# The first v load behind the first pair's q, and block sums spread by a sum over one number

## The chip, the cores and the metric

The kernel runs on one core of a Trainium2 chip. The metric is device time in microseconds (us) from launch to end, as the median of several runs. Beside it there is the profile of one execution, whose span counts from the first to the last instruction; the launch around it is not in the span.

The engines go by their names in the profile: PE is TensorE (PEld its weight loads), DVE is VectorE, ACT is ScalarE, POOL is GpSimd, SP is SyncE. SP, ACT and POOL issue the transfers (DMAs). Each engine works through its own instructions in their order and waits at semaphores for the others.

## The reference

Attention over blocks, and behind it an MLP mixer. q, k and v are 4 batches x 8 heads x 768 rows x 64. Of each head, the keys are cut into 12 blocks of 64, and a query attends to its own block and to the three blocks with the highest gate scores, causally:

```python
k_rep = k.reshape(B, H, n_blocks, block, D).mean(axis=3)
gate_scores = np.einsum('bhsd,bhnd->bhsn', q, k_rep)
...
top_idx = np.argsort(gate_scores, axis=-1)[..., -top_k:]
...
scores = np.where(mask, scores, -1000000000.0)
...
return np.matmul(attn, v).astype(np.float32)
```

The heads stand side by side as x, 768 x 512 for each batch. A token mixer follows (`h = relu(xt @ w_tok1) @ w_tok2`, `u = x + h^T`) and a channel mixer (`u + relu(u @ w_ch1) @ w_ch2`).

## The kernel before, in words

The work is done by pairs of heads, 16 in all (`pair(p)`, L482), four to a batch; behind each four come the two big products of the channel mixer (`mlp(b)`, L815). A pair goes through these steps:

- **Loads.** k and q of a pair, as f32, by SP; for pair 0 half of them by ACT, and in two halves of the rows (L516). v by POOL (L525), which makes f16 of it on the way, into the tile VA. A buffer of VA is one of five.
- **k.** TensorE transposes it (L446, `transposed`), VectorE sums each block of 64 columns (L553, `tensor_reduce` over a tile in PSUM) into ks3, 12 sums for each of the 64 numbers of a head. `spread` (L532 to L534) copies these sums, for each of the two heads, into ks2b, where a head's sums stand in columns of their own with zeros elsewhere; it is two copies of 64 partitions x 12 (pair 0: four of 64 x 6). The planner gives them to DVE or to POOL. From pair 6 on (`thirds`) `split` does this in another way, and `spread` is not used.
- **q.** TensorE transposes it (L446), ACT or DVE writes QT from PSUM (L342 or L344, the two lines of the helper `copy`), in two halves, (QT, 0) and (QT, 1). An f16 copy goes to QA (L344, L342).
- **Gate.** TensorE multiplies QT with ks2b (L639), VectorE adds the causal bias (L643), takes the greatest (L670) and compares (L683), and the own block is set by a memset (L690). What comes out, bn, is transposed (L710) and copied as 12 more rows into QA.
- **Scores and output.** L731 multiplies KA with QA, L744 (ACT) takes the exponential E, L752 (POOL) masks the diagonal blocks, L761 multiplies with VA.
- **Mixers.** L779 and L793 the token mixer, L827 and L849 the channel mixer.

No order of instructions is written by hand. Each step is given to a planner (`Plan`, L88) with its cost on each engine that could do it, what it reads and writes, and a due time `pr`. `Plan.run` (L129) is a list scheduler: it starts what can start first, by its own clock, and among what can start within 30 ns of that the one with the lowest `pr`. A transfer is not started until the planner's own count of the transfers under way is within 3 us (`AHEAD`) of being through, and not while another with a lower `pr` could go. The due times come from the table `L` (L53): for k, q and v of the first four pairs `ekd`, `eqd` and `evd`, taken from the pair's time `T(p) + L["o" + p]`. For pair 0 that time is -2.69, for pair 1 it is 5.78 + 2.1 = 7.88, for pair 2 it is 11.56 + 2.23. The instructions are then written out in the order of the planned starts, and it is that order by which each engine goes; when an instruction really starts is settled on the chip by its semaphores. Where TensorE would stand idle early on, the planner puts in filler matmuls on zeros (L899), their number fixed at build time.

The load of v has no input but its buffer, so in the program nothing but its place on POOL holds it back:

```python
P.op({"POOL": (1100.0, 2200.0, 1536 * 16.0 / 16)}, lambda: nc.gpsimd.dma_start(...),
     wr=[(VA, 0)], pr=t0 - lead["vd"], not_before=5000.0)
```

`not_before` is a bound of the planner's clock alone. `warm` is a tile of one number for each partition, which ACT writes once at the start (L520).

Of the kernel before, what the change touches and what calls it, by code (L numbers as in the profile page):

```python
# [13 lines left out]
ALU = mybir.AluOpType  # L14
AX = mybir.AxisListType
# [284 lines left out]
def kernel(  # L300
# [11 lines left out]
    nc = tc.nc  # L312
    B, H, S, D = q.shape
# [20 lines left out]
    def sb(shape, dt, name):  # L334
        return sp.tile(shape, dt, tag=name, name=name)
# [10 lines left out]
    P = Plan()  # L346
    ENG = {"PE": nc.tensor, "ACT": nc.scalar, "DVE": nc.vector, "POOL": nc.gpsimd, "SP": nc.sync}
# [39 lines left out]
    warm = sb([128, 1], FP, "warm")  # L387
# [40 lines left out]
    def weights(after):  # L428
        weight("w1", w1, moe_w_tok1.rearrange("(j p) t -> p j t", p=128), 768, 60, L["w1"], after)
        weight("w2", w2, moe_w_tok2.rearrange("(g p) s -> p g s", p=128), 256, 135, L["w2"], after)  # L430
        for c in range(NCC):
            weight(("wc1", c), wc1[:, c, :], moe_w_ch1[128 * c:128 * c + 128, :], 128, 247, L["wc1"] + c, after)
        for f in range(0, NFC, 3):
            weight(("wc2", f), wc2[:, f:f + 3, :], moe_w_ch2[128 * f:128 * f + 384, :].rearrange("(g p) c -> p g c", p=128),
                   384, 98, L["wc2"] + f / 3, after)


    def T(p):
        return EARLY * min(p, PPB) + PACE * max(0, p - PPB)
# [24 lines left out]
    def halves(i):  # L464
        return slice(HS * i, HS * i + HS)

    def upper(t):

        return t.bitcast(BF).rearrange("c (n two) -> c n two", two=2)[:, :, 1]
# [12 lines left out]
    def pair(p):  # L482
        b, c = divmod(p, PPB)
        h = 2 * c
        step = T(p + 1) - T(p)
        t0 = T(p) + L[f"o{p}"]
        thirds = p >= L["th"]
        cut = p < CUT
        lead = {n: L["e" + n if p < PPB else n] for n in LEADS}
# [5 lines left out]
        def at(i, lead):  # L495

            return t0 - lead - (L["cu"] if cut and i == 0 else 0.0)

        def loaded(t, i):
            return [(t, (x, i)) for x in range(2)] if cut else [(t, f) for f in range(4)]  # L500
        q32, k32 = Buf(q32r), Buf(k32r)
        qs, ks_, vs = q[b, h:h + 2], k[b, h:h + 2], v[b, h:h + 2]
        QA, KA, VA, QT = Buf(QAr), Buf(KAr), Buf(VAr), Buf(QTr)
        for t, src, name in ((k32, ks_, "kd"), (q32, qs, "qd")):
            e = "SP"
            if straight_k if t is k32 else straight_q:
                for f in range(4):
                    P.op({e: (570.0, 1600.0, 768 * 13.0 / 16)}, lambda f=f, t=t, src=src, e=e: ENG[e].dma_start(
                        out=t.t.rearrange("p j x d -> p (j x d)")[32 * f:32 * f + 32].rearrange("t (g i) -> t g i", i=32),
                        in_=src[f // 2, :, 32 * (f % 2):32 * (f % 2) + 32].rearrange("(g t) i -> t g i", t=32)), wr=[(t, f)], pr=t0 - lead[name])  # L510
                continue
            for x in range(2):
                e = "ACT" if p == 0 and x else "SP"
                for i in range(1 + cut):
                    n = NJ // (1 + cut)
                    P.op({e: (520.0 if p == 0 else 570.0, 1600.0, 128 * n * 17.6 / 16)}, lambda x=x, t=t, src=src, e=e, i=i, n=n: ENG[e].dma_start(  # L516
                        out=t.t[:, n * i:n * i + n, x, :], in_=src[x, 128 * n * i:128 * n * i + 128 * n].rearrange("(j p) d -> p j d", p=128)),
                        wr=[(t, (x, i) if cut else x)], pr=t0 - lead[name] - (199.0 - 20.0 * i + lead[name] if p == 0 else 0.0))
        if p == 0:
            P.op({"ACT": (1500.0, 1600.0)}, lambda: nc.scalar.activation(out=warm, in_=zero[:, 0:1], func=AF.Exp), pr=-98.0)  # L520
        if p < 3:
            e = "SP" if p else "ACT"
            P.op({e: (450.0, 1600.0, 24 * 135 / 16)}, lambda e=e: ENG[e].dma_start(out=KA.t[64:KR], in_=indc), wr=[(KA, "ind")],
                 pr=t0 - lead["qd"] + 0.2 if p else -99.0)
        P.op({"POOL": (1100.0, 2200.0, 1536 * 16.0 / 16)}, lambda: nc.gpsimd.dma_start(  # L525
            out=VA.t[:, :, :, 0:64], in_=vs.rearrange("x (j p) d -> p x j d", p=128)), wr=[(VA, 0)], pr=t0 - lead["vd"], not_before=5000.0)


        ks2b = kp = Buf(kppr if thirds else ksr)
        ks3 = Buf(ks3r)  # L530

        def spread(e, z):  # L532
            for x in range(2):
                ENG[e].tensor_copy(out=ks2b.t[64 * x:64 * x + 64, x, z], in_=ks3.t[64 * x:64 * x + 64, 0, z])  # L534

        if straight_k:
            KT = Buf(KTr)
            for i in range(2):
                P.op({"DVE": (487.0, 570.0)}, lambda i=i: nc.vector.transpose(
                    out=KT.t[:, halves(i)], in_=k32.t.rearrange("p j x d -> p (j x d)")[:, halves(i)]), rd=loaded(k32, i), wr=[(KT, i)], io="S0>S0", pr=t0 - L["ku"])  # L540
            P.op({"DVE": (862.0, 945.0)}, lambda: nc.vector.tensor_reduce(
                out=ks3.t[:, 0], in_=KT.t.rearrange("c (n w) -> c n w", w=64), axis=AX.X, op=ALU.add), rd=[(KT, 0), (KT, 1)], wr=[(ks3, 0), (ks3, 1)], io="S0>S0", pr=t0 - lead["kr"])
# [3 lines left out]
            if not thirds:  # L546
                P.op({"POOL": (380.0, 450.0), "DVE": (160.0, 240.0)}, lambda e: spread(e, slice(0, NB)), rd=[(ks3, 0), (ks3, 1)], wr=[(ks2b, 0), (ks2b, 1)], pr=t0 - lead["kr"] + 0.1, io="S0>S0 S2>S2")
        else:
            k16 = Buf(k16r)
            for i in range(2):  # L550
# [3 lines left out]
                    out=ks3.t[:, 0, 6 * i:6 * i + 6], in_=t.t[:, 0:HS].rearrange("c (n w) -> c n w", w=64),  # L554
                    axis=AX.X, op=ALU.add), rd=[(t, 0)], wr=[(ks3, i)], io="P0>S0", pr=at(i, lead["kr"]))
                if not thirds and (cut or i == 1):
                    z = slice(6 * i, 6 * i + 6) if cut else slice(0, NB)
                    P.op({"POOL": (380.0, 450.0), "DVE": (160.0, 240.0)}, lambda e, z=z: spread(e, z), rd=[(ks3, i)] if cut else [(ks3, 0), (ks3, 1)],
                         wr=[(ks2b, i)] if cut else [(ks2b, 0), (ks2b, 1)], pr=at(i, lead["kr"]) + 0.1, io="S0>S0 S2>S2")
# [17 lines left out]
        if dual:  # L577
            k16 = Buf(k16r)
            P.op({"POOL": (778.0, 828.0)}, lambda: nc.gpsimd.tensor_copy(
                out=k16.t.rearrange("p (j c) -> p j c", c=128), in_=k32.t.rearrange("p j x d -> p j (x d)")), rd=loaded(k32, 0), wr=[(k16, 0)], io="S0>S0", pr=t0 - L["k16"])  # L580
# [13 lines left out]
        for i in range(2):  # L594
            if straight_q:
                P.op({"DVE": (487.0, 570.0)}, lambda i=i: nc.vector.transpose(
                    out=QT.t[:, halves(i)], in_=q32.t.rearrange("p j x d -> p (j x d)")[:, halves(i)]), rd=loaded(q32, i), wr=[(QT, i)], io="S0>S0", pr=t0 - L["qu"])
# [7 lines left out]
            if thirds:  # L605
                a, z = (128, HS) if i == 0 else (HS, S)
                P.op(dve(z - a), lambda t=t, i=i, a=a, z=z: nc.vector.tensor_tensor(
                    out=R1.t[:, a - 128:z - 128], in0=t.t[:, a - HS * i:z - HS * i], in1=upper(QT.t[:, a:z]), op=ALU.subtract),
                    rd=[(t, 0), (QT, i)], wr=[(R1, i)], io="P0S0>S0", pr=t0 - L["r"])
        if straight_q and thirds:  # L610
            P.op({"POOL": (1207.0, 1257.0), "DVE": (745.0, 828.0)}, lambda e: ENG[e].tensor_tensor(
                out=R1.t, in0=QT.t[:, 128:S], in1=upper(QT.t[:, 128:S]), op=ALU.subtract), port=True, rd=[(QT, 0), (QT, 1)], wr=[(R1, 0), (R1, 1)], io="S0>S0", pr=t0 - L["r"])
        if p == 0:
            weights((QT, 0))
        for x in range(2):
            for i in range(1 + cut):
                n = NJ // (1 + cut)
# [12 lines left out]
        if not thirds:  # L630
            if cut:
                P.op({"POOL": (100.0, 150.0)}, lambda: nc.gpsimd.memset(gm.t[:, 0:2].rearrange("p j (x n) -> p j x n", n=NB)[:, :, :, 6:NB], -1.0e9), wr=[(gm, 9)], pr=t0 - lead["g"] - 9.0)
            for i, (z0, z1) in enumerate(parts):
# [3 lines left out]
                def gate(z0=z0, z1=z1, nb=nb):  # L637
# [6 lines left out]
                    out=cols(gm.t[:, z0:z1]), in0=g.t[:, W2 * z0:W2 * z1].rearrange("p (j w) -> p j w", w=W2)[:, :, 0:2 * nb].rearrange("p j (x n) -> p j x n", n=nb),  # L644
                    in1=cols(gbias[:, z0:z1]), op=ALU.add), rd=[(g, i)] + ([(gm, 9)] if cut else []), wr=[(gm, i)], io="P0S0>S0", pr=at(i, lead["g"]) + 0.1)
        else:
            P.op({"POOL": (1207.0, 1257.0)}, lambda: nc.gpsimd.tensor_tensor(out=R2.t, in0=R1.t, in1=upper(R1.t), op=ALU.subtract),
                 rd=[(R1, 0), (R1, 1)], wr=[(R2, 0)], io="S0>S0", pr=t0 - L["r"] + 0.1)
# [9 lines left out]
            for i in range(3):  # L658
                P.op({"DVE": (202.0, 283.0)}, lambda i=i: nc.vector.tensor_tensor(out=gm.t, in0=gv(2 - i), in1=(gm.t if i else gbias), op=ALU.add),
                     rd=[(g, 0)], wr=[(gm, 0)], io="P0S0>S0", pr=t0 - lead["g"] + 0.1)  # L660

        for i, (z0, z1) in enumerate(parts):
# [10 lines left out]
            if thirds:  # L673
                P.op({"DVE": (92.0, 174.0)}, lambda z0=z0, z1=z1, third=third: nc.vector.tensor_copy(out=third(), in_=m8.t[:, z0:z1, :, 2:3]),
                     rd=[(m8, i)], wr=[(g, (3, i))], io="S0>P0", pr=at(i, lead["g"]) + 0.25)
# [17 lines left out]
        if p >= L["bd"]:  # L693
            bnt = Buf(bntr)
            P.op({"DVE": (487.0, 570.0)}, lambda: nc.vector.transpose(  # L695
                out=bnt.t.rearrange("p j x n -> p (j x n)"), in_=bn.t.rearrange("p j x n -> p (j x n)")), rd=bn_all, wr=[(bnt, 0)], io="S0>S0", pr=t0 - lead["b"])
# [24 lines left out]
        for x in range(2):  # L721
# [34 lines left out]
            def av(a=a, E=E, x=x):  # L756
# [8 lines left out]
                out=rc.t.rearrange("p n o -> p (n o)"),  # L765
                in_=a.t[:, 0:NJ * 65].rearrange("p (j d) -> p j d", d=65)[:, :, 64:65].rearrange("p n o -> p (n o)")),
                rd=[(a, 0)], wr=[(rc, 0)], io="P0>S0", pr=t1 + 1.3)
            P.op(dve(384), lambda a=a, rc=rc, x=x: nc.vector.tensor_tensor(  # L768
                out=xp.t[:, :, 64 * x:64 * x + 64], in0=a.t[:, 0:NJ * 65].rearrange("p (j d) -> p j d", d=65)[:, :, 0:64],
# [6 lines left out]
        def tok1():  # L776
# [8 lines left out]
            rd=[(m1, 0)], wr=[(h1, 0)], io="P0>S0", pr=t2 + 0.1)  # L785
        u, uT = u_of[b], uT_of[b]
        for i, (j0, n) in enumerate([(0, 3), (3, 3)]):
            m = Buf(Rr)

            def umix(m=m, j0=j0, n=n):  # L790
# [6 lines left out]
                out=u.t[:, c, j0:j0 + n, :], in0=xp.t[:, j0:j0 + n, :], in1=m.t[:, 0:128 * n].rearrange("p (j d) -> p j d", d=128), op=ALU.add),  # L797
                rd=[(m, 0), (xp, 0), (xp, 1)], wr=[(u, (c, i))], io="P0S0>S0", pr=t2 + 0.3)
# [66 lines left out]
    for b in range(B):  # L865
        for c in range(PPB):
            pair(PPB * b + c)
        mlp(b)
# [74 lines left out]
```

## Time and profile before

| | us |
|---|---|
| median of 3 runs | 246.92 (246.72 to 247.88) |
| the profiled execution | 246.32 |
| its span | 244.6 |
| DVE busy | 170.4 |
| ACT busy | 160.6 |
| POOL busy | 128.2 |

The profiled execution took 246.32 in all, 1.7 more than its span. A row of the timeline reads: start, duration, engine, line, operation, out<-in, form, how many, and in brackets how long the engine was idle before it and what ended that. DMA rows give a queue's packets, its MB and the time of its packets as a share of 16 engines. The core's transfers move 30.82 MB in 124120 packets, 117652 of them under 512 B. The granted clock of TensorE is 1.00 throughout.

### The profile page before, as it was taken

Reading aid. Unit: us, or ns where it says so; the run is one execution under the profiler, and the core shown is the slowest. Engines: PE = TensorE matmul, PEld = TensorE weight load, DVE = VectorE, ACT = ScalarE, POOL = GpSimd, SP = SyncE. Lnnn points to the kernel's source line nnn. Section 1 sums busy time; section 2 is a strip of 40 time slices with the busy share of each in tenths; the row PEclk is TensorE's granted clock in tenths of the full one; section 3 lists DMA queues with packets and bytes.
Section 4 is the critical chain, followed back from the end, with each engine's and each line's share of the span. In section 5 each row is a group of like instructions: output and inputs, shape, how many; then the busy total and the mean of one; then the engine's idle time right before and its main releaser. Section 6 shows DMA issues by size and latency. Waiting matters only on the chain.

```text
span 244.6 us, 6642 instructions
## 1 busy us (share of the span) xinstructions
PE 238.1 (97%) x2467; PEld 162.9 (67%) x2467; DVE 170.4 (70%) x546; ACT 160.6 (66%) x251; POOL 128.2 (52%) x263
## 2 busy tenths in 40 slices
PE   7799999999999999999999999999999999999995
PEld 7588878897656676567575666567755766554644
DVE  3889887877879999999999889968385632202112
ACT  3786978759587696788988675589724672360620
POOL 6188778878487583978796747676102110000000
DMA  8999999999899897879999899510213211112103
GB/s 158 201 203 215 207 171 182 173 132 177 133 83 168 158 148 142 186 150 178 161 138 168 186 166 126 151 53 3 64 46 111 79 32 46 43 43 86 46 18 110
DMA packets 124120, 30.82 MB, mean 126 GB/s; under 512 B 117652, under 2 KB 120596, under 8 KB 124088
## 3 DMA queue, kind: packets, MB, share of 16 engines
q1 hardware_dynamic: 94400, 22.89, 46.7%
q0 software_dynamic: 28064, 7.08, 32.8%
q10 hardware_dynamic: 1624, 0.43, 0.9%
q8 instruction: 19, 0.31, 0.6%
q14 instruction: 13, 0.11, 0.2%
HBM read 29.01 MB, written 8.45 MB: 153 GB/s over the span
## 4 chain that ended last, share of the span: by engine, by line
PE 91%; DMA 3%; DVE 3%; issue 0%; SPq 0%; POOL 0%; POOLq 0%
PE pm L827 26%; PE pm L849 25%; PE sc L731 14%; PE pm L761 9%; PE pm L779 4%; PE pm L793 4%; DMA k<-in_k_dram 3%; PE pm L639 2%; PE pm L654 2%; PE pm L446 2%; PE pm L710 1%; PE pm L899 1%; DVE ks L553 1%; DVE ks L534 1%; PE pm L807 1%; DVE m L670 1%
## 5 line engine op out<-in xcount | busy, mean ns | idle before, releaser
L744 ACT ACTIVATE E<-sc 128x1024 f16<-128x1024 f32 (+2 forms) x96 | 84.0, 917 | 22.7 <-PE sc L731 21.3
L827 PE MATMUL pm<-uT,wc 128*128 128x384 f16 x384 | 69.9, 326 | 0.0
L849 PE MATMUL pm<-wc,h 128*128 128x512 f16 (+2 forms) x312 | 68.8, 363 | 0.0
L752 POOL TENSOR_SCALAR_AFFINE_SELECT E<-E 128x256 f16<-128x256 f16 (+1 forms) x96 | 39.2, 416 | 43.2 <-ACT E L744 41.4
L835 ACT ACTIVATE h<-pm 128x384 f16<-128x384 f32 x71 | 34.5, 491 | 28.2 <-PE pm L827 28.0
L827 PEld LDWEIGHTS <-wc 128*128 128x128 f16 x384 | 36.0, 98 | 22.5
L731 PE MATMUL sc<-QA,KA 76*128 76x512 f16 (+3 forms) x264 | 48.2, 301 | 0.3 <-DVE QA L344 0.3
L849 PEld LDWEIGHTS <-h 128*128 128x128 f16 x312 | 28.4, 98 | 26.0
L853 DVE TENSOR_TENSOR os<-u,pm 128x512 f32<-128x512 f16 (+2 forms) x26 | 16.6, 640 | 33.9 <-PE pm L849 33.2
L731 PEld LDWEIGHTS <-KA 76*128 76x128 f16 x264 | 23.6, 98 | 14.5 <-issue 0.4
L761 PEld LDWEIGHTS <-E 128*128 128x128 f16 x672 | 24.9, 98 | 3.6
L761 PE MATMUL pm<-VA,E 128*128 128x65 f16 x672 | 26.1, 193 | 0.0
L796 DVE TENSOR_TENSOR u<-x,pm 128x384 f16<-128x384 f16 x32 | 16.5, 542 | 4.7 <-PE pm L793 4.7
L837 DVE TENSOR_SCALAR h<-pm 128x384 f16<-128x384 f32 x25 | 13.8, 554 | 8.5 <-PE pm L827 7.5
L768 DVE TENSOR_TENSOR x<-pm,rc 128x384 f16<-128x384 f32 x32 | 17.8, 555 | 0.9
L525 POOL DMA_DIRECT2D VA<-in_v_dram x16 | 16.8, 1051 | 0.4 <-issue 0.3
L793 PE MATMUL pm<-h,w 128*128 128x128 f16 x192 | 13.8, 219 | 0.0
L342 ACT COPY QA<-bnt 12x384 f16<-12x384 f16 x20 | 10.2, 508 | 5.3 <-DVE bnt L695 4.9
L670 DVE MAX8 m<-gm 128x8 f32<-128x12 f32 x160 | 13.2, 156 | 0.5
L779 PE MATMUL pm<-x,w 128*128 128x128 f16 x192 | 13.3, 219 | 0.0
L793 PEld LDWEIGHTS <-w 128*128 128x128 f16 x192 | 11.9, 98 | 1.9
L779 PEld LDWEIGHTS <-w 128*128 128x128 f16 x192 | 11.7, 98 | 2.0 <-DVE x L768 0.4
(79 smaller groups left out, 302.2 us busy)
## 6 DMA issues: line engine op xcount, KB each, us to landing
out_dram<-os SPq DMA_DIRECT2D x22, 256.0 KB, 2.5
q<-in_q_dram SPq DMA_DIRECT2D x42, 96.0 KB, 2.9
k<-in_k_dram SPq DMA_DIRECT2D x38, 96.0 KB, 3.8
VA<-in_v_dram POOLq DMA_DIRECT2D x16, 192.0 KB, 6.0
wc<-in_moe_w_ch_dram POOLq DMA_DIRECT2D x8, 384.0 KB, 6.6
k<-in_k_dram SPq DMA_DIRECT2D x12, 192.0 KB, 5.6
turn<-k SPq DMA_DIRECT2D x11, 192.0 KB, 2.1
uT<-turn SPq DMA_DIRECT2D x44, 48.0 KB, 2.0
```

What stands on the lines that cost most here:

```text
L525: P.op({"POOL": (1100.0, 2200.0, 1536 * 16.0 / 16)}, lambda: nc.gpsimd.dma_start(out=VA.t[:, :, :, 0:64], in_=vs.rearrange("x (j p) d -> p ...
L731: nc.tensor.matmul(out=s.t[:, at:at + 128 * m], lhsT=KA.t[:, x, 128 * kk:128 * kk + 128], rhs=QA.t[:, q0:q0 + m, x, :], start=True, stop=True)
L744: nc.scalar.activation(out=E.t[:, BASE[g_]:BASE[g_ + 1]], in_=s.t[:, 0:WIDTH[g_]], func=AF.Exp, scale=scale)
L752: nc.gpsimd.affine_select(out=o, in_=o, pattern=[[0, len(d)], [1, 128]], compare_op=ALU.is_ge, fill=0.0, base=0, channel_multiplier=-1)
L761: nc.tensor.matmul(out=t[:, jq, :], lhsT=E.t[:, cc:cc + 128], rhs=VA.t[:, x, kk, :], start=(kk == 0), stop=(kk == jq))
L768: P.op(dve(384), lambda a=a, rc=rc, x=x: nc.vector.tensor_tensor(out=xp.t[:, :, 64 * x:64 * x + 64], in0=a.t[:, 0:NJ * 65].rearrange("p (j ...
L779: nc.tensor.matmul(out=m1.t[:, 128 * t:128 * t + 128], lhsT=w1[:, j, 128 * t:128 * t + 128], rhs=xp.t[:, j, :], start=(j == 0), stop=(j == ...
L793: nc.tensor.matmul(out=m.t[:, 128 * j:128 * j + 128], lhsT=w2[:, t, 128 * (j0 + j):128 * (j0 + j) + 128], rhs=h1.t[:, t, :], start=(t == 0 ...
L827: nc.tensor.matmul(out=m.t[:, 0:HS], lhsT=wc1[:, c, 128 * f:128 * f + 128], rhs=uT.t[:, c].rearrange("p (a w) -> p a w", a=4)[:, :, 96 * i ...
L835: nc.scalar.activation(out=o, in_=w, func=AF.Relu)
L849: nc.tensor.matmul(out=m.t[:, 0:wide], lhsT=h2.t[:, f, 128 * jj:128 * jj + 128], rhs=wc2[:, f, w:w + wide], start=(f == 0), stop=(f == NFC ...
L853: P.op(dve(wide), lambda j=j, m=m, o=o, w=w, wide=wide: nc.vector.tensor_tensor(out=o.t[:, w:w + wide].rearrange("p (c d) -> p c d", d=128 ...
```

## The change

Two edits. The step that loads v moves behind those that make QT. For pair 0 it now begins with a copy by POOL of one number, the last of QT's first row, into `warm`; the load stands behind that copy on POOL, and in the planner the step reads (QT, 1) and costs 70 ns more. For other pairs the load is as it was. And where VectorE does the spreading, the two copies become two `tensor_reduce` that sum over a last axis of one number; where POOL does it, it is the copy as before. The table `L` is as it was.

```diff
-        P.op({"POOL": (1100.0, 2200.0, 1536 * 16.0 / 16)}, lambda: nc.gpsimd.dma_start(
-            out=VA.t[:, :, :, 0:64], in_=vs.rearrange("x (j p) d -> p x j d", p=128)), wr=[(VA, 0)], pr=t0 - lead["vd"], not_before=5000.0)
...
         def spread(e, z):
             for x in range(2):
-                ENG[e].tensor_copy(out=ks2b.t[64 * x:64 * x + 64, x, z], in_=ks3.t[64 * x:64 * x + 64, 0, z])
+                if e == "DVE":
+                    nc.vector.tensor_reduce(out=ks2b.t[64 * x:64 * x + 64, x, z], in_=ks3.t[64 * x:64 * x + 64, 0, z].rearrange("c (n w) -> c n w", w=1), axis=AX.X, op=ALU.add)
+                else:
+                    nc.gpsimd.tensor_copy(out=ks2b.t[64 * x:64 * x + 64, x, z], in_=ks3.t[64 * x:64 * x + 64, 0, z])
...
+        def vload():
+            if p == 0:
+                nc.gpsimd.tensor_copy(out=warm[0:1, 0:1], in_=QT.t[0:1, S - 1:S])
+            nc.gpsimd.dma_start(out=VA.t[:, :, :, 0:64], in_=vs.rearrange("x (j p) d -> p x j d", p=128))
+        P.op({"POOL": (1100.0 + 70.0 * (p == 0), 2200.0, 1536 * 16.0 / 16)}, vload, rd=[] if p else [(QT, 1)], wr=[(VA, 0)], pr=t0 - lead["vd"], not_before=5000.0)
         if p == 0:
             weights((QT, 0))
```

## The prediction

> **What bounds the kernel now.** I read the page first, for the share of each engine and the chain that ended last, then the windows, the chain of waits and the timeline of the first 24 us.
>
> ```profile
> PE 238.1 (97%) x2467; PEld 162.9 (67%) x2467; DVE 170.4 (70%) x546; ACT 160.6 (66%) x251; POOL 128.2 (52%) x263
> ...
> PE 91%; DMA 3%; DVE 3%; issue 0%; SPq 0%; POOL 0%; POOLq 0%
> ```
>
> TensorE is busy for 97% of the span and makes 91% of the chain. So there are two ways to a shorter kernel: less work on TensorE, which this change doesn't touch, or letting its dense run begin sooner. The windows show where that run begins.
>
> ```profile
> 0.00:10.00 10.00, 7.40 (x68) 6.63 (x69) 5.43 (x28) 5.14 (x11) 3.75 (x21) 1.00 1.13 172
> ...
> 20.00:200.00 180.00, 179.90 (x2020) 124.86 (x2017) 148.29 (x473) 133.24 (x199) 117.14 (x229) 1.00 0.93 137
> ```
>
> The first columns are the stretch, its length and TensorE's busy time. Of the first 10 us TensorE is busy for 7.40, and from 20 to 200 for 179.90 of 180. What moves ahead of some 20 us moves the whole rest, as long as nothing new makes TensorE wait. So the question is what holds the first 20 us. The chain of waits of 0 to 30 us tells it.
>
> ```profile
> 4.15 5.64 DMA k<-in_k_dram
> ...
> 12.14 0.53 DVE ks L534
> ...
> 12.69 0.90 DVE ks L534
> 13.58 0.27 DVE QA L344
> ...
> 13.89 0.98 PE sc L731 x7
> 14.87 1.04 PE pm L639 x10
> ```
>
> First the k of pair 1 (4.15 + 5.64: it lands at 9.79), then VectorE's block sums and their spreading (L534: 0.53 and 0.90), then one VectorE copy (13.58), and only then the scores at 13.89 and the gate of pair 1 (L639) behind them. The timeline shows what lies beside them.
>
> ```profile
> 3.31 1.19 POOL L525 DMA_DIRECT2D VA<-in_v_dram  x1
> ...
> 7.79 0.47 ACT L342 COPY QT<-pm 128x384 f32<-128x384 f32 x1
> ...
> 8.37 1.92 SPq L516 DMA_DIRECT2D k<-in_k_dram  x2
> ...
> 8.66 0.55 DVE L344 CAST QA<-QT 64x384 f16<-64x384 f32 x1
> ...
> 9.28 0.30 PE L710 MATMUL pm<-id,bn 128*64 128x128 f16 x2
> ...
> 9.93 0.84 PE L446 MATMUL pm<-id,k 128*128 128x128 f32 x6 [0.35 <-DMA k<-in_k_dram]
> ...
> 11.27 0.32 PE L899 MATMUL pm<-zero 128*128 128x120 f16 x3
> 11.31 0.29 POOL L690 MEMSET bn<- 64x6 f16 x2 [6.81 <-DVE bn L683]
> ...
> 11.79 0.82 POOL L344 COPY KA<-k 64x768 f16<-64x768 f16 x1 [0.19 <-DVE k L344]
> ...
> 12.14 1.44 DVE L534 COPY ks<-ks 64x12 f32<-64x12 f32 x2
> ...
> 12.18 0.52 PE L446 MATMUL pm<-id,q 128*128 128x128 f32 x3 [0.59 <-DMA q<-in_q_dram]
> 12.56 0.99 POOL L752 TENSOR_SCALAR_AFFINE_SELECT E<-E 128x384 f16<-128x384 f16 x2
> ...
> 12.63 0.36 PE L710 MATMUL pm<-id,bn 128*64 128x128 f16 x3
> ...
> 12.92 0.55 PE L446 MATMUL pm<-id,q 128*128 128x128 f32 x3
> ...
> 13.30 0.27 PE L899 MATMUL sc<-zero 128*128 128x120 f16 x2
> ...
> 13.50 0.72 DVE L344 COPY QA<-pm 12x384 f16<-12x384 f16 x2
> ...
> 15.74 0.85 PE L446 MATMUL pm<-id,k 128*128 128x128 f32 x6
> ...
> 17.25 0.83 PE L761 MATMUL pm<-VA,E 128*128 128x65 f16 x21
> ...
> 18.10 0.48 DVE L534 COPY ks<-ks 64x12 f32<-64x12 f32 x2
> ```
>
> TensorE waits for transfers twice: 0.35 us for pair 1's k at 9.93 and 0.59 us for its q at 12.18. VectorE's two spreading copies (12.14) take 1.44 us: the first ends at 12.67 and the second at 13.58, just after GpSimd's copy (11.79 + 0.82 = 12.61) and its two masks (12.56 + 0.99 = 13.55) end.
>
> **The load, part by part.** What does the first v load take from others? The transfers by queue, of 4 to 6, of 6 to 8 and of 10 to 12 us (packets, MB, share of 16 engines):
>
> ```profile
> q0 software_dynamic: 31, 0.00, 3.0%
> ```
> ```profile
> q0 software_dynamic: 1337, 0.17, 132.2%
> q1 hardware_dynamic: 580, 0.14, 48.7%
> ```
> ```profile
> q1 hardware_dynamic: 1585, 0.43, 134.7%
> ```
>
> q0 is GpSimd's queue, q1 SyncE's. Issued at 3.31, the load has moved 31 packets by 6 us, so its first come some 2.6 us after the issue, and 1337 in the next 2 us, in which q1 moved 580; without v, q1 moves 1585 in 2 us. So v displaces 1005 packets of q1, which is 1005 / 792 per us = 1.27 us. These are the packets of pair 1's k and q. Pair 0's own k and q were on their way before v's packets came, so I give pair 0 no gain: the second half of its QT is still written at 7.79 + 0.47 = 8.26.
>
> With the change GpSimd's copy starts near 8.3. Its price isn't in the trace; by that engine's rows it lies between one of the two small memsets of L690 (0.29 / 2) and the 64x768 copy (0.82). I take 0.15, by the nearer, and little depends on it: GpSimd is idle for 6.81 us ahead of L690 at 11.31, and the copy and the issue (1.19) end at 9.6. What is queued behind the waiting copy is that L690, which needs VectorE's result of some 11 us in any case. No DMA on another queue waits behind it. So the edit itself costs nothing; were that idle time gone, it would be the wait and 0.15.
>
> Pair 1's k then lands at 9.79 - 1.27 = 8.5. But TensorE is busy until 9.28 + 0.30 = 9.58, so the transposes go from 9.93 to 9.6: **0.3 us**. VectorE's sums follow the transposes, so the spreading starts at 11.85 in place of 12.14. Pair 1's q, for which TensorE waited until 12.18, lands 1.27 sooner too, at some 10.8: v, 2.6 us behind its issue of 8.45, comes in only at 11. TensorE then starts on q when its filler matmuls end, 11.59 - 0.3 = 11.3: **0.9 us** sooner. L710 behind it moves from 12.63 to 11.7 and ends at 12.1.
>
> **The spreading.** Its durations, and those of sums on VectorE:
>
> ```profile
> L534 DVE COPY ks<-ks x12: 152/168/896, 5.4 to 27.8; 64x12 f32<-64x12 f32 x8, 64x6 f32<-64x6 f32 x4
> ```
> ```profile
> L541 DVE TENSOR_REDUCE ks<-KT 128x12 f32<-128x768 f32 x9 | 8.5, 942 | 0.3
> L553 DVE TENSOR_REDUCE ks<-pm 128x6 f32<-128x384 f32 x14 | 7.3, 549 | 4.1 <-PE pm L446 4.1
> ```
> ```profile
> L541 DVE TENSOR_REDUCE ks<-KT x9: 910/943/954, 71.8 to 153.9; 128x12 f32<-128x768 f32 x9
> ```
>
> An undisturbed copy takes 152 to 168 ns, the worst 896. What would a sum over one number of 12 take? L541 and L553 differ by 384 numbers and 393 ns, so about 1 ns a number and a fixed 150: 12 numbers make some **165 ns**, as the copy. The bounds are that fixed part and a whole L553, 150 and 549; at 549 the spreading would end at 12.95, and half a microsecond of the gain would be gone. What I count on is that it doesn't wait for GpSimd. L541 reads SBUF as the new sums do, and GpSimd is busy for 52% of the span, yet all nine stay within 910 to 954. So a pair takes 0.33 in place of 1.44, and ends at 11.85 + 0.33 = 12.2 in place of 13.58.
>
> **The sum.** VectorE's QA copy needs L710 (12.1) and the end of the spreading (12.2); half of 0.72 later it releases the scores, at 12.6. TensorE comes to them after the second half of q (12.92 + 0.55, now 12.0 to 12.55) and two filler matmuls, at 12.7 to 12.8, in place of 13.89: **1.1 us**. Each part alone gives some 0.3: with the load alone the copies still sit behind GpSimd's masks, which end 0.3 sooner (13.25); with the sums alone L710 still waits for q, and TensorE is free at 13.57. From 13.89 on everything is computing and follows at the same distance; the spreading of pair 2 (18.10, 0.48 in place of 0.33) lies on the chain and adds some 0.1. The later ones lie beside a full TensorE and give nothing. **In all 1.2 us**, bounded by 0.3 below (only one part works) and 1.5 above (q's whole 1.27 and more of the later spreading).
>
> What is late next? **v itself**, for L761 at 17.25, now wanted at 16.1. And pair 2's k (issued at 8.37), for L446 at 15.74, now wanted at 14.5.
>
> ```profile
> k<-in_k_dram SPq DMA_DIRECT2D x2, 192.0 KB, 4.8
> ```
> ```profile
> VA<-in_v_dram POOLq DMA_DIRECT2D x1, 192.0 KB, 6.9
> ```
> ```profile
> DMA to landing us min/median/max: 4.2/6.0/9.3
> ```
>
> v took 6.9 us when first issued; from 8.45 it lands at 15.35, 0.75 ahead of need. Pair 2's k took 4.8 us in the median from its two issues (8.37 and shortly after), so the second lands before 14; it is issued sooner now but shares with v from 11 on, and comes out the same, some 0.5 ahead of need. What v displaces there falls on loads for which nobody waits.
>
> The Trainium skill, "SBUF — State Buffer", section "SBUF: two separate sides", speaks against the new place: descriptors of a load issued by GpSimd can't be written while VectorE runs an operation that takes the shared port pair. The row at 8.66, VectorE's cast (0.55), lies in the new issue. By that rule v could land 0.55 later, at 15.9, and still be in time; by the row itself the cast runs at some 1 ns a number, as the sums do, and the landing stays at 15.35. No row of this trace shows a load held up so. The sum is 1.2 by both.
>
> **The order** on the engines is written by the planner. The load's due time, -2.69 - 9.12 = -11.8, stood behind those of pair 1's k (7.88 - 26.02 = -18.1), q (-16.2) and pair 2's k (-12.2) already, so the planner had placed it late; the chip merely issued it as soon as GpSimd was free. The new dependency need not move anything else.
>
> **Rivals.**
> 1. *v lands late* (slower). With the 9.3 us of the slowest load it lands at 8.45 + 9.3 = 17.75, and TensorE stands at L761 until then, 0.5 us later than before: 247.4. It decides from a landing after 17.25. For it: only 0.75 us of slack. Against: beside a full q1 it took 6.9 the first time, the median is 6.0, and 9.3 is the worst of 16. Chance 0.11.
> 2. *The sums wait for GpSimd as the copies did*, or q doesn't come sooner: 0.3 us, 246.6. Against it the nine L541. Chance 0.14.
> 3. *The transfers take it back*: pair 2's k lands up to 0.6 after its new need, which leaves 0.6 us: 246.3. For it: q1 is as full from 10 to 12 as ever. Chance 0.12.
> 4. *The change doesn't do what it says*, the planner's order moves after all, here or far behind: some us either way, more likely slower, 248.2 to 249. Against it the due times above. Chance 0.08.
>
> **How the numbers follow.** The profiled execution took 246.32 (span 244.6); with 1.2 less, 245.1 and 243.4. The median of the runs shown is 246.92, 0.6 above it, and I predict against that: 246.92 - 1.2 = **245.7**, chance 0.55, by itself 245.3 to 246.2. The range reaches to rivals 1, 2 and 3 and to the upper bound of the gain with the spread of the runs: 244.9 to 247.4. About 0.5% (1.23 us) is what a measurement of this kernel can tell from no change. The forecast lies on that bound (245.69): 0.41 of its 0.55 I give to more than it, since the spreading of the later pairs may add to the 1.2, and 0.01 of rival 4. Faster 0.42; slower by more than 0.5% 0.11 (0.07 of rival 4, and 0.04 of rival 1, with a landing after 18.5); the same 0.47, the rest of all cases.
>
> **What would show it.** Right: the first L525 near 8.4; L446 on pair 1's k with no wait for a transfer; both L534 together 0.33 at some 11.85, beside GpSimd's copy; the scores of 13.89 at 12.7 to 12.8; L761 of 17.25 at about 16.1 with no wait for VA; the span 243.4. Wrong: a wait of L761 for in_v_dram, L534 over 0.3 us each, or L446 of pair 2 waiting for k. The prediction fails if TensorE's dense run from 20 us on shows new gaps, or if v's packets take more from q1 at 11 us than they took at 6.

## The result and the profile after

The changed kernel takes **244.66 us** (median of 6 runs, 244.35 to 244.96) against 246.82 for the kernel before in the same 6 rounds (246.49 to 247.88). The ratio is 0.9898, with a 95% interval of 0.9873 to 0.9923: 1.0% faster, 2.16 us between the medians. The profiled execution took 244.40 with a span of 242.7, so 1.9 less than before in both. The forecast was 245.7 and the range ended at 244.9: the direction was right, the gain is almost twice the forecast, and the time lies outside the range.

In some executions of either kernel TensorE's granted clock falls to half early on (e3 and e8 below show it and its price): by a mean clock of 0.993 or less that is so in 60 of the 92 executions of the kernel before that were timed beside the experiments, and in 2 of 20 of the changed kernel. The profiles of e3, e5, e8 and e14 have such a fall, and they are read ahead of it, save where the text says so.

The page of the changed kernel, busy time by engine and the shares of the chain that ended last:

```profile
PE 237.5 (98%) x2467; PEld 162.6 (67%) x2467; DVE 168.7 (70%) x546; ACT 160.4 (66%) x251; POOL 128.8 (53%) x264
...
PE 96%; DVE 2%; issue 0%; POOL 0%; DVEq 0%; POOLq 0%
```

No transfer is in the chain any more; before, DMA made 3% of it. The chain of waits of the changed kernel's first 30 us (start, length, what):

```profile
4.05 0.35 PE pm L446 x3
...
4.42 0.57 DVE ks L553
...
7.41 0.40 DVE m L675 x4
...
8.16 0.82 PE pm L644 x6
...
9.21 0.81 PE pm L446 x6
10.02 0.67 PE sc L736 x10
10.69 0.16 PE pm L904 x3
10.85 0.34 PE pm L446 x3
...
12.05 0.96 PE sc L736 x7
13.02 1.03 PE pm L644 x10
...
15.56 0.67 PE pm L766 x21
```

From 4.05 it goes from TensorE's own first transposes through pair 0's VectorE work and stays on VectorE and TensorE. The timeline of the changed kernel has the steps (after the start and the duration: engine, line, what; the lines are shifted, the load is L616 now):

```profile
3.85 0.54 PE L446 MATMUL pm<-id,k 128*128 128x128 f32 x3
...
4.42 0.56 DVE L553 TENSOR_REDUCE ks<-pm 128x6 f32<-128x384 f32 x1 [2.62 <-PE pm L446]
...
7.99 0.18 POOL L615 COPY warm<-QT 1x1 f32<-1x1 f32 x1 [4.62 <-ACT QT L342]
...
8.23 1.20 POOL L616 DMA_DIRECT2D VA<-in_v_dram  x1
...
9.14 0.88 PE L446 MATMUL pm<-id,k 128*128 128x128 f32 x6
...
10.68 0.50 PE L446 MATMUL pm<-id,q 128*128 128x128 f32 x3
...
11.03 0.82 POOL L344 COPY KA<-k 64x768 f16<-64x768 f16 x1 [0.18 <-DVE k L344]
...
11.39 0.33 DVE L532 TENSOR_REDUCE ks<-ks 64x12 f32<-64x12 f32 x2
...
11.81 0.99 POOL L757 TENSOR_SCALAR_AFFINE_SELECT E<-E 128x384 f16<-128x384 f16 x2
...
12.04 0.98 PE L736 MATMUL sc<-QA,KA 76*128 76x384 f16 x7
...
15.39 0.83 PE L766 MATMUL pm<-VA,E 128*128 128x65 f16 x21
```

The load is issued at 8.23. Pair 1's k and q (9.14, 10.68) begin without the waits of 0.35 and 0.59 us. Both sums of pair 1 take 0.33 us, with GpSimd's copy (11.03 to 11.85) beside them all along, and end before its masks begin. The scores of 13.89 start at 12.04, the first product with VA at 15.39 in place of 17.25. The transfers, of 6 to 8 us in the changed kernel, then those issued near 8.25 (KB each, us to landing):

```profile
q1 hardware_dynamic: 1657, 0.42, 123.2%
```
```profile
VA<-in_v_dram POOLq DMA_DIRECT2D x1, 192.0 KB, 6.5
```

q1 moved 1657 packets in these 2 us where it had moved 580 beside v. And v landed 6.5 us after its issue, at 14.75, 0.64 ahead of L766.

A part of the 1.85 us by which the scores came sooner is at the very start. These are the kernel before's rows that answer to the first two of the timeline above:

```profile
3.85 0.85 PE L446 MATMUL pm<-id,k 128*128 128x128 f32 x3
...
4.74 0.56 DVE L553 TENSOR_REDUCE ks<-pm 128x6 f32<-128x384 f32 x1 [2.94 <-PE pm L446]
```

TensorE's three first transposes took 0.85 us before and 0.54 now, and so the first block sum came at 4.74 and 4.42. Nothing in the program differs up to there but the load on GpSimd, which was issued at 3.31; whether that did it was left to the experiments.

### The profile page after: what moved, and what is told of

It is laid out like the page before. It is cut to its first block, busy times and chain, and to the rows that moved or that the text cites. A ratio compares the mean times of both kernels' runs of the same rounds, so it can differ in the third digit from the quotient of the medians.

```text
span 242.7 us, 6643 instructions
## 1 busy us (share of the span) xinstructions
PE 237.5 (98%) x2467; PEld 162.6 (67%) x2467; DVE 168.7 (70%) x546; ACT 160.4 (66%) x251; POOL 128.8 (53%) x264
## 4 chain that ended last, share of the span: by engine, by line
PE 96%; DVE 2%; issue 0%; POOL 0%; DVEq 0%; POOLq 0%
PE pm L832 26%; PE pm L854 26%; PE sc L736 15%; PE pm L766 9%; PE pm L784 4%; PE pm L798 4%; PE pm L446 3%; PE pm L644 3%; PE pm L904 2%; PE pm L659 2%; PE pm L715 1%; PE pm L812 1%; DVE m L675 1%; DVE ks L553 0%; PE sc L904 0%
## 5 line engine op out<-in xcount | busy, mean ns | idle before, releaser
L766 PEld LDWEIGHTS <-E 128*128 128x128 f16 x672 | 24.9, 98 | 3.6
L766 PE MATMUL pm<-VA,E 128*128 128x65 f16 x672 | 26.2, 193 | 0.0
L616 POOL DMA_DIRECT2D VA<-in_v_dram x16 | 16.9, 1054 | 0.4 <-issue 0.2
L784 PE MATMUL pm<-x,w 128*128 128x128 f16 x192 | 13.3, 219 | 0.0
```

What stands on the lines that cost most here:

```text
L616: nc.gpsimd.dma_start(out=VA.t[:, :, :, 0:64], in_=vs.rearrange("x (j p) d -> p x j d", p=128))
L766: nc.tensor.matmul(out=t[:, jq, :], lhsT=E.t[:, cc:cc + 128], rhs=VA.t[:, x, kk, :], start=(kk == 0), stop=(kk == jq))
L784: nc.tensor.matmul(out=m1.t[:, 128 * t:128 * t + 128], lhsT=w1[:, j, 128 * t:128 * t + 128], rhs=xp.t[:, j, :], start=(j == 0), stop=(j == ...
```

## The experiments

Theory A: the load gives q1 back to pair 1's k and q, the sums free VectorE of GpSimd, and neither is worth much alone, since either leaves the other wait in place; with both gone, the chain runs through pair 0's VectorE work, and what shifts that shifts the end. Rivals: B, the load is nearly all; C, the parts add up; D, the early load held up pair 0 before; E, some executions are slower because TensorE's clock falls back, a question beside the others.

| | kernel | median us | ratio to before, 95% interval | span of its profile |
|---|---|---|---|---|
| e1 | load alone | 246.99 | 1.0009 (0.9979 to 1.0038) | 244.2 |
| e2 | sums alone | 246.27 | 0.9988 (0.9961 to 1.0014) | 243.9 |
| e3 | changed, once more | 246.21 (1 run) | | 244.5 |
| e4 | before, once more | 246.08 (1 run) | | 244.4 |
| e5 | before, VectorE dose in a gap | 246.77 | 1.0008 (0.9979 to 1.0037) | 248.0 |
| e6 | changed, the same dose | 244.56 | 0.9897 (0.9866 to 0.9928) | 242.6 |
| e7 | changed, more fillers | 245.00 | 0.9921 (0.9892 to 0.9951) | 243.2 |
| e8 | changed, timed | 244.72 | 0.9907 (0.9876 to 0.9937) | 246.0 |
| e9 | load behind the first half of q | 244.72 | 0.9909 (0.9885 to 0.9933) | 242.7 |
| e10 | load 1.5 us later | 246.03 | 0.9950 (0.9922 to 0.9978) | 244.7 |
| e11 | spreading by tensor_scalar | 247.41 | 0.9995 (0.9954 to 1.0035) | 244.1 |
| e12 | changed, timed | 244.58 | 0.9891 (0.9859 to 0.9923) | 242.6 |
| e13 | changed, VectorE dose without a gap | 246.11 | 0.9972 (0.9935 to 1.0009) | 243.3 |
| e14 | before, the same dose | 247.15 | 1.0004 (0.9974 to 1.0035) | 245.4 |

### e1 and e2: one part each

e1 is the changed kernel with the old spreading, e2 the kernel before with the new one:

```diff
# e1, against the changed kernel
-                if e == "DVE":
-                    nc.vector.tensor_reduce(...)
-                else:
-                    nc.gpsimd.tensor_copy(...)
+                ENG[e].tensor_copy(out=ks2b.t[64 * x:64 * x + 64, x, z], in_=ks3.t[64 * x:64 * x + 64, 0, z])
# e2, against the kernel before: the same lines the other way round
```

> The load waits for q, the spreading stays two copies on VectorE. Theory A (the two parts need each other: with the load alone the copies of pair 1 still stand behind GpSimd's copy and masks): 0.3 to 0.6 us faster than before, the spreading of pair 1 still over 1 us long. Rival B (the load is nearly the whole gain, since it is what TensorE waited for at 9.93 and 12.18): 1.2 us faster or more. Rival C (the parts add up, half each): about 1 us.

> Sums in place of the copies, the load issued at once as before. Theory A: 0.3 to 0.5 us faster than before, since pair 1's q still lands at 12.05 and L710 behind it; the sums 0.33 together at some 12.1. Rival B: nothing to 0.3. Rival C: about 1 us. If the copies' wait was the whole matter: 1.2 us or more.

The timeline of e1:

```profile
10.93 0.50 PE L446 MATMUL pm<-id,q 128*128 128x128 f32 x3
...
11.63 1.44 DVE L531 COPY ks<-ks 64x12 f32<-64x12 f32 x2
...
13.38 0.81 PE L733 MATMUL sc<-QA,KA 76*128 76x384 f16 x6 [1.08 <-DVE QA L344]
```

Pair 1's q is there at 10.93, 1.25 us sooner than before, yet the copies still take 1.44 us, and the scores start at 13.38 after a wait of 1.08 us for VectorE. Of the load's 1.25 us no more than 0.5 reaches the scores. The timeline of e2:

```profile
11.79 0.33 DVE L535 TENSOR_REDUCE ks<-ks 64x12 f32<-64x12 f32 x2
...
12.07 0.52 PE L446 MATMUL pm<-id,q 128*128 128x128 f32 x3 [0.82 <-DMA q<-in_q_dram]
...
13.31 0.98 PE L734 MATMUL sc<-QA,KA 76*128 76x384 f16 x7
```

Here the sums take their 0.33, and TensorE stands 0.82 us for pair 1's q at 12.07. Again the scores come at 13.3, and not at 12.04. In the medians neither is told from the kernel before (e1 ±0.3%, e2 0.1% faster, ±0.3%), while both together give 1.0%: **B falls**. But the medians hide a part, since the clock fell in 9 of the 12 executions of e1, in 6 of the 12 of e2 and in 14 of the 23 of the kernel before beside them. Where it stayed up, the medians are 246.00 (e1, 3 executions), 245.70 (e2, 6) and 246.46 (before, 9), against 244.67 (18) of the changed kernel in the result, e8 and e12. So each part alone is worth some 0.5 and 0.8 us and both at once some 1.8, and **C falls too**, if less clearly: by these few executions two thirds of the gain add up. The rest is that of removing two waits of which either is enough to hold the scores at 13.3 or later.

### e3, e4 and e8: the same two kernels again, and the clock

> The changed kernel once more, for a second profile. Theory A with the clock: the first block sum of VectorE comes at 4.42 or up to 0.4 later, by when TensorE's transposes begin to run fast, and the scores of pair 0 (12.04 in the first profile) and the span (242.7) move with it one for one. Rival D (the early issue of v is what held pair 0 up by 0.3 before): the first sum at 4.42 again each time.

> The kernel before once more, for a second profile. Theory A with the clock: the first block sum at 4.42 to 4.75, but the transposes of pair 1's k stay at 9.9, because they wait for a transfer, and the span stays at 244.6 to 245.2 whichever it is. Rival D: the first sum at 4.74 again.

> The changed kernel unaltered, timed beside the others. Theory E: its times fall into two groups, one at 244.4 to 245 and one 1.5 to 2 us above it; the fastest 1.7 to 2 us below the fastest of before. Rival: one group round 244.7.

**My expectation for e4 missed in one point.** Pair 1's k came without a wait in it:

```profile
9.51 0.88 PE L446 MATMUL pm<-id,k 128*128 128x128 f32 x6
...
12.27 0.52 PE L446 MATMUL pm<-id,q 128*128 128x128 f32 x3 [1.05 <-DMA q<-in_q_dram]
...
13.51 0.98 PE L731 MATMUL sc<-QA,KA 76*128 76x384 f16 x7
```

So the wait for k of the first profile (0.35 us) isn't in every execution of the kernel before. The wait for q is, as far as the traces with the full clock go: 0.59 in the first profile, 1.05 here, 0.82 in e2, which has the early load too. Measured from this execution, the scores of e1 and e2 come only 0.1 to 0.2 us sooner.

The changed kernel's first sum came at 4.74 in e3, as in e4. So the load didn't cause the difference of 0.32: **D falls**. What differs is when TensorE begins to run fast. In the first profile of the changed kernel it did so at its first transposes, in that of the kernel before some 0.7 us later. But the span of e3 is 244.5 for another reason. Its stretches (length, TensorE busy, and after the five engines the granted clock), then those of e8, then one of the first profile of the changed kernel:

```profile
6.10:9.50 3.40, 2.71 (x27) 2.24 (x25) 2.97 (x15) 2.54 (x6) 1.10 (x2) 1.00 1.34 219
...
9.50:12.80 3.30, 3.30 (x23) 3.12 (x22) 2.67 (x13) 2.29 (x5) 1.47 (x5) 0.50 1.65 195
```
```profile
5.80:9.20 3.40, 2.59 (x27) 2.23 (x25) 3.13 (x14) 2.73 (x7) 0.77 (x2) 1.00 1.34 224
9.20:16.00 6.80, 6.80 (x41) 5.38 (x41) 3.88 (x17) 3.99 (x9) 3.39 (x7) 0.50 1.54 202
```
```profile
7.40:10.80 3.40, 2.71 (x30) 2.50 (x29) 2.99 (x18) 2.98 (x8) 1.56 (x4) 1.00 1.35 211
```

From 9.5 on TensorE's clock stands at 0.50 for 3.3 us in e3; in e8 for 6.8 us, and that execution took 247.72 where the other six took 244.42 to 244.88. How busy TensorE was ahead of it doesn't decide it: 2.71 of 3.40 us in e3 and 2.59 in e8, but 2.71 as well in the first profile of the changed kernel and 2.48 in e4 (5.8 to 9.2), where the clock stayed up. What decides stays open. So e3 is 1.8 us above the first profile by the clock, not by the change. The Trainium skill, "TensorE: Matmul & The Clock Gate", section "Part 1: The HAM clock gate", says that the gate looks at TensorE's work in windows of some 3.4 us that run on regardless of the program, so that the moment of the switch varies; both traces agree: the clock is at half for about one such window in e3 and for two in e8, from 9.5 in the one and from 9.2 in the other.

### e7: more fillers

```diff
+        if n == 7:
+            n = 19
```

> The changed kernel with 19 filler matmuls where there were 7 (at 6.95 us, where TensorE then stood for 0.69 us). Theory E (some executions are 1.5 to 2 us slower because TensorE's clock falls to 0.5 for 3.4 us after a thin stretch at 6 to 9 us): fewer or no such executions, the median 0.3 to 1 us below that of the changed kernel, the fastest the same. Rival: the same spread of times, since the thin stretch isn't what decides, or 0.1 to 0.5 slower since the fillers are in the way.

None of six runs stands out (244.81 to 245.54), but of the unaltered kernel's 20 runs in the result, e3, e8 and e12 only two do: too few to say that the fillers prevent it. The fastest is 0.4 above e8's; in its profile the clock rose late (first sum at 4.74) and v landed at 15.84, just late for its product. Inconclusive, and no better.

### e5, e6, e13 and e14: is pair 0's VectorE work the bound now?

e5 and e6 put a sum over 192 numbers of the transposed k behind the first block sum, e13 and e14 one over 256 numbers of QT behind the cast to QA; the result goes to a tile that nobody reads:

```diff
+                        nc.vector.tensor_reduce(out=extra, in_=t.t[:, 0:192].rearrange("c (n w) -> c n w", w=64), axis=AX.X, op=ALU.add)
...
+                    if p == 0 and i == 0 and e == "DVE":
+                        nc.vector.tensor_reduce(out=extra, in_=QT.t[:, 0:256].rearrange("c (n w) -> c n w", w=64), axis=AX.X, op=ALU.add)
```

> The kernel before with 0.35 us more on VectorE in pair 0 (a sum over 192 numbers into a tile that nobody reads, behind the first block sum). Theory A (before, the chain runs through the transfer of pair 1's q, and pair 0's VectorE work is hidden behind it): same as before within 0.3 us; pair 1's q still lands at about 12. Rival (pair 0's VectorE work was the bound in both): 0.35 slower.

> The changed kernel with the same 0.35 us more. Theory A (with both edits the chain runs through pair 0's VectorE work): 0.35 us slower than the changed kernel, every step behind it later by that much, and VectorE's sums of pair 1 too. Rival: nothing, if the transfers still set the pace.

In e6 nothing was lost, but the dose had failed: VectorE waits there for its own sum in any case, and the spreading began 0.74 us behind the first sum in place of 0.67, so 0.07 later. Both say nothing on the question.

> The changed kernel with 0.4 us more on VectorE in pair 0, now where its instructions stand without a gap: a sum over 256 numbers into a tile that nobody reads, behind the cast of the first half of QT to QA (6.04). Theory A (with both edits pair 0's VectorE work sets the pace): pair 1's transposes of k and q, the scores and the end come 0.3 to 0.4 us later, by the same distance from the first block sum: median 244.9 to 245.1. Rival (the transfers or TensorE's own order set it): 244.6 to 244.7, q at 6.3 us behind the first sum as before.

> The kernel before with the same sum at the same place. Theory A (before, the landing of pair 1's q sets the pace and pair 0's VectorE work is hidden): the transposes of q still start at 12.1 to 12.3, and the time is that of before within 0.2 us. Rival: 0.3 to 0.4 us slower, as the changed kernel.

e13, block sum, dose, and the transposes of pair 1's q:

```profile
4.74 0.56 DVE L554 TENSOR_REDUCE ks<-pm 128x6 f32<-128x384 f32 x1 [2.94 <-PE pm L447]
...
6.85 0.40 DVE L628 TENSOR_REDUCE extra<-QT 128x4 f32<-128x256 f32 x1
...
11.36 0.50 PE L447 MATMUL pm<-id,q 128*128 128x128 f32 x3
```

From the first sum to pair 1's q it is 10.68 - 4.42 = 6.26 us in the first profile of the changed kernel, 6.29 in e7 and 6.25 in e10, whenever that sum came, and 11.36 - 4.74 = 6.62 in e13: the dose arrives with 0.33 us. In the kernel before the distance isn't fixed. There q starts at 12.1 to 12.3 whether the first sum came at 4.56 (e5) or 4.74, because the transfer lands then: at 12.05 in the first profile, 12.13 in e4 and 11.94 in e5, where the clock had fallen at 11 already. **So pair 0's VectorE work sets the pace after the change and didn't before**, and an early rise of the clock is worth its 0.33 us only now. In time e13 is no clean measure: its fastest four runs are 244.94 to 244.97, 0.5 above the fastest of e8, but the other eight reach to 247.96, and its median is 1.4 us above e8's, more than the dose. In those eight the clock fell: their mean clock is 0.993 or 0.986, as in the profiles of e3 and e8, and 0.998 or more in the four. Why it fell more often here no run shows. e14 gave the time of before within 0.35%, which is twice the dose and settles little; in its three executions with the clock up it took 246.23 to 246.40, where the kernel before beside it has a median of 246.34 (9 executions), as theory A says. In its profile the clock fell at 10.3, so its trace isn't used.

### e9 and e10: where the load stands

```diff
# e9
-                nc.gpsimd.tensor_copy(out=warm[0:1, 0:1], in_=QT.t[0:1, S - 1:S])
+                nc.gpsimd.tensor_copy(out=warm[0:1, 0:1], in_=QT.t[0:1, 0:1])
# e10
+                for _ in range(3):
+                    nc.gpsimd.memset(idle, 0.0)
```

> The changed kernel with the one-number copy reading the first half of QT (written at 6.0) instead of the second: the load is issued some 1.7 us sooner, near 6.5, and its packets come from 9.1 on. Theory A (what counts is that pair 1's q is through before v's packets come): q's second part lands at about 11.5 in place of 10.3, the transposes of q start at 11.6 in place of 10.7, and 0.7 to 1.0 us of the gain is gone: 245.4 to 245.7. Rival (any delay of the load does, since the k of pair 1 is what matters): as the changed kernel, 244.7.

> The changed kernel with three memsets (some 0.4 us each) between the one-number copy and the load on GpSimd: the load is issued some 1 us later, at 9.2 to 9.4. Theory A (v is next: it lands at 14.75 and is wanted at 15.39): it lands at 15.7 to 16.1, the first product with VA starts at 15.8 to 16.1 and 0.3 to 0.7 us are lost: 245.0 to 245.4. Rival (v lands when the transfers of the others let it, and later issue costs nothing): 244.7.

**My expectation for e9 missed.** The load was issued at 6.74, and pair 1's q still started at 10.72. The transfers of e9, from 9 to 10 us and from 10 to 11:

```profile
q1 hardware_dynamic: 721, 0.20, 123.8%
q0 software_dynamic: 69, 0.01, 17.5%
```
```profile
q0 software_dynamic: 954, 0.12, 218.2%
q1 hardware_dynamic: 165, 0.04, 30.5%
```

v's packets came near 10 us, some 3.2 us after the issue and not 2.6, and by then q was all but through (it landed at 10.32). So the change has 1.5 us of room towards an earlier load, and with it v lands at 13.24, 2.2 us ahead of need in place of 0.64. The time is the same as e12's within the spread.

e10 came out stronger than expected. Its timeline:

```profile
9.73 1.20 POOL L619 DMA_DIRECT2D VA<-in_v_dram  x1
...
17.26 0.82 PE L769 MATMUL pm<-VA,E 128*128 128x65 f16 x21 [1.39 <-DMA VA<-in_v_dram]
```

Issued 1.5 us later than in the changed kernel (the memsets took 1.36), v landed 7.5 us on, and TensorE stood 1.39 us for it. The time is 1.3 to 1.5 us above e8 and e12. So rival 1 of the prediction is a real mechanism that sits 0.6 us away.

### e11: which operations wait for GpSimd

```diff
-                    nc.vector.tensor_reduce(...)
+                    nc.vector.tensor_scalar(out=ks2b.t[64 * x:64 * x + 64, x, z], in0=ks3.t[64 * x:64 * x + 64, 0, z], scalar1=0.0, scalar2=None, op0=ALU.add)
```

> The changed kernel with the spreading by a sum with the number 0 (tensor_scalar) in place of the sum over one number. Theory A (it is the kind of operation that waits for GpSimd, and this one waits as the copies do): the two of pair 1 take over 1 us, the scores start 1.3 us later, 246.0 to 246.4, as with the load alone. Rival (only the copies wait, or they waited for something else): 0.33 together and 244.7.

```profile
11.20 0.82 POOL L344 COPY KA<-k 64x768 f16<-64x768 f16 x1 [0.18 <-DVE k L344]
...
11.56 1.44 DVE L532 TENSOR_SCALAR ks<-ks 64x12 f32<-64x12 f32 x2
...
11.98 0.99 POOL L757 TENSOR_SCALAR_AFFINE_SELECT E<-E 128x384 f16<-128x384 f16 x2
...
13.31 0.98 PE L736 MATMUL sc<-QA,KA 76*128 76x384 f16 x7 [1.09 <-DVE QA L344]
```

In e11's timeline the two take 1.44 us, just as the copies, and end where GpSimd's masks end (11.98 + 0.99 = 12.97); the scores wait 1.09 us for VectorE; the median is that of e1 and of the kernel before within the spread. It isn't the copy as such: of three operations with the same operands two wait for GpSimd and the sum doesn't. The Trainium skill, "VectorE: DVE Perf Modes", section "The perf-mode tier table", gives tensor_copy and tensor_scalar a faster mode for f32 in SBUF and tensor_reduce none; which of these waited here fits it.

## Why the prediction was wrong, step by step

- **What bounds it**: right. The gain came ahead of 20 us, and the dense run behind moved whole: the scores by 1.85, the first product with VA by 1.86, the span by 1.9.
- **The load**: right in mechanism and size. q1 got 1077 more packets from 6 to 8 us (I had said 1005); pair 1's q landed at 10.32 (I had said 10.8), and k and q no longer wait. But the wait for k, which I counted with 0.3 us, is missing from one execution of the kernel before (e4). The order of the other instructions stayed. VectorE's cast beside the issue held up nothing that shows: the issue took 1.20 us, against 1.19 before.
- **The sums**: right, 0.33 for 0.33, and that each part alone gives little. In the medians of e1 and e2 the 0.3 us that I gave them drowns; with the clock up they gave 0.5 and 0.8.
- **v late**: it landed at 14.75 (I said 15.35) and was wanted at 15.39 (16.1). The room of 0.64 us was sized right, and e10 shows the price beyond it; it isn't there in every execution, since in e7 v took 7.3 us and landed only as it was needed. That the packets come 2.6 us behind the issue didn't hold: some 3.4 in the changed kernel (its first 17 packets are of 11.5 to 11.8) and 3.2 in e9.
- **The step that failed is the way from 9.58 to the scores at 12.75**, in two terms. The first is "TensorE is busy until 9.28 + 0.30 = 9.58": I took the end of pair 0's work from one execution and treated it as a fixed floor, with "I give pair 0 no gain". The load gives it none indeed (e3). But the floor became the bound, and it moves with the clock: the first sum came 0.32 us sooner in the profiled execution of the changed kernel. The kernel before could hardly profit from that, since its q landed at 12 whenever the first sum came (e5).
- **The second term is the overlap of matmuls**, which I put at nothing. With 0.33 taken off for the clock, the scores stand at 12.37, and I had 12.75. I had let TensorE start each group where the last one's displayed duration ended. The chain shows that matmuls overlap: the three fillers at 10.69 count 0.16 us there, where I had let 0.32 pass. That this term is there without an early rise of the clock too is shown by e10, whose first sum came at 4.74, as before, and whose scores start at 12.35; in e7 it is so as well:

```profile
12.38 0.98 PE L736 MATMUL sc<-QA,KA 76*128 76x384 f16 x7
```

- The sum of the profiles: for the scores 1.14 forecast (13.89 to 12.75), 0.33 by the clock and 0.38 by the overlap make the 1.85 measured. Behind them the span gained less than 0.1 more, where I had given 0.1 to the spreading of pair 2. That the profiled execution had the early rise of the clock was luck: e12's (first sum 4.42) and e9's (4.46) had it, those of e3, e7, e8 and e10 (4.74 to 4.77) not. In the median there is probably little of its 0.33, though no trace shows that run by run: of the changed kernel's 18 times without a fall in the result, e8 and e12, six lie at 244.34 to 244.50 and twelve at 244.62 to 244.96.
- **The base of the forecast was off as well.** The medians differ by 2.16, and I had taken 1.2 off a median, 246.92, as if the clock would fall as often after the change. It fell in 60 of 92 executions of the kernel before and in none of the six of the result. With the clock up the medians are 246.40 (32 executions) and 244.67 (18), 1.7 apart; the other 0.4 or so fits the falls, if they were as frequent in the result's six executions of the kernel before, whose clocks aren't on record. Why they are rarer after the change stays open. My upper bound of 1.5 counted the waits of the old chain and not what the new one gains by; so the range was too short.

## What to carry to other kernels

Where two waits end close together, an edit that removes one of them can drown in the spread, as both did here in the medians; compare executions with the same granted clock, and try the edits together before either is thrown away. When both go, ask what the new chain consists of and whether it is fixed: what one execution shows of an engine off the path is a sample, not a floor. A first-needed transfer can be bought by holding back one that is needed late, but look for its new landing against its first use, since 1.5 us more of delay gave back 1.3 us.

## What the runs showed of the hardware

TensorE's clock can fall to half soon after it has risen: 3.3 us at 0.50 in e3 and 6.8 us in e8, at a price of 1.5 and 3.0 us (their spans less 242.7 and the 0.33 of the late rise), though TensorE was busy for 2.71 and 2.59 of the 3.40 us ahead. Whether an execution has it isn't decided by the program alone, since the same kernel shows both, but the program shifts how often: 60 of 92 before, 2 of 20 after the change. The small operations that spread 12 numbers had medians of 156 to 169 ns on VectorE, whichever of the three was used; copies and tensor_scalar took up to 896 and 894 when they waited for GpSimd, sums never more than 163. And VectorE's wait for its own result hid a 0.35 us instruction but for 0.07.
